# A gated mix of a state-space scan and a long convolution: issue order and buffer places planned by a list schedule in the builder, in place of tile pools and the library's scheduler

## The chip, the cores and the metric

The kernel runs on one core of one Trainium2 chip. The metric is the device time of the whole program in microseconds (us); smaller is better. Every number below comes from runs on such a chip or from the profile of one of them. A profiled execution has a "span", which is about 2 us shorter than the device time.

The core has five engines that issue independently. PE multiplies matrices (PEld is its weight load, which overlaps the multiplying), DVE is the vector engine, ACT the scalar engine, POOL a general engine that is slower at the elementwise work here (a 128x1024 bf16 multiply takes about 2.2 us on POOL and 0.68 us on DVE), and SP issues DMA transfers. In the traces each engine works its instructions off in the order in which they were put into its queue: two kernels below that have the same plan show the same 595 DVE instructions in the same order, and likewise for PE, ACT and SP. "POOL's queue" or "SP's queue" also stands for the DMA queue that this engine feeds. "Granted clock" (PEclk) is the share of full speed that PE was allowed.

## The reference

The inputs are `x`, `k`, `v` of 2048 × 1024 in bf16 (the argument `q` is ignored; `x` takes its place), the scan's parameters, and a convolution kernel of length 2048 for each of 1024 channels. Condensed, it computes:

```python
g = sigmoid((x * gate_w).sum(-1, keepdims=True))
# a: diagonal complex recurrence, P = 1024 states
Bu = x @ B_bar^T
h  = Lam_bar * h + Bu[t]          # for t in range(2048)
a  = 2 * real(h @ Cmat^T) + x * Dskip
# b: 4-tap shift convolution, product, long convolution of length 2048 by FFT
kv = shift_conv(k, shift_k) * v
b  = x * (causal_conv(kv, ssm_k) + kv * ssm_D)
out = g * a + (1 - g) * b
```

## The kernel before

The work has three kinds of pieces.

- **Scan**, 8 blocks of 128 states: prepare the block of B (`prep`), multiply it with x for odd and even rows (`gemm_u`), rotate, scan and rotate back on DVE (`rot`), then recover the odd rows on PE (`odd`). Each finished block of states, "H", two pieces of 512 KB, is stored to DRAM.
- **Convolution**, 8 units of 128 channels: a four-tap product on DVE (`kv_steps`), then a three-stage DFT on PE (`stage1`, `spec`, `inverse`), a complex `product` on DVE in the middle, and `final`, whose result is multiplied by x·(1−g) and stored to DRAM as `pB`.
- **Outputs**, 16 row tiles × 2 halves of the columns ("dh"): 16 matmuls each of H with C, then two DVE instructions that add x·Dskip and pB. Half 0 needs the convolution of units 0 to 3 alone, half 1 that of units 4 to 7.

PSUM, the matmul's result memory, is one pool with two 2-bank buffers for the scan (`psS`) and two for the convolution (`psB`). SBUF is a set of tile pools. The two halves of the program are Python generators. They are interleaved by a weight, and the library's scheduler settles each engine's final order.

```python
psum = ctx.enter_context(tc.tile_pool(name="psum", bufs=2, space=bass.MemoryType.PSUM))
pX = tc.tile_pool(reuse_waits="tile", name="pX", bufs=1, side="right")     # xT: all of x, transposed
...
def prep(pi, bn):
    dg = sp.tile([128, 6, 128], BF16, name="dg", bufs=3)
    for j, cf in enumerate(dcoef):                                         # six DVE instructions
        TS(out=dg[:, j, :], in0=ident, scalar1=col(cf, pi), scalar2=None, op0=ALU.mult)
...
# at the end of the scan: the right-hand pools are closed, a new one is opened in their place
pK.__exit__(None, None, None)
pS.__exit__(None, None, None)
pX.__exit__(None, None, None)
pC = tc.tile_pool(reuse_waits="tile", name="pC", bufs=1, side="right")
...
for pi in order:
    load_CT(0, pi)                                                         # two DMA transposes of C each
    Hs[pi] = cp.tile([128, NC, 2, 2, CW], BF16, name=f"Hr{pi}")
    for c in range(NC):
        nc.sync.dma_start(out=Hs[pi][:, c].rearrange("p a b s -> p (a b s)"), in_=h_scr[pi, c])
...
# one output tile
nc.gpsimd.tensor_tensor(out=xn, in0=xn, in1=dsk[:, ds_], op=ALU.mult)      # POOL
...
STT(out=pb, in0=xn, scalar=gc, in1=pb, op0=ALU.mult, op1=ALU.add)          # DVE
STT(out=ot, in0=ps[:, ti, :], scalar=gc, in1=pb, op0=ALU.mult, op1=ALU.add)
...
TOT_S, TOT_C = 190.0, 123.0
for w in sg:                                                               # the interleaving
    done_s += w
    while cg is not None and done_c < TOT_C * done_s / TOT_S:
        ...
```

## Time and profile before

The kernel before took 605.7 us (median of its first 3 runs, 603.29 to 607.32). These line numbers help with the profiles:

| piece | line before | line after |
|---|---|---|
| `prep`, PE | L235 | L750 |
| `gemm_u` | L261 | L785 |
| `odd` | L313 | L855 |
| DFT stage 1 / spec / inverse / final, PE | L563 / L573 / L593 / L617 | L633 / L647 / L673 / L695 |
| complex product, DVE, four instructions | L582, L583, L585, L586 | L660 to L663 |
| x·(1−g), POOL | L608 | L687 |
| x·Dskip, POOL | L429 | L961 |
| output matmuls; the DVE pair after them | L434; L440, L441 | L982; L970, L988 |

The page gives the busy time of each engine and its share of the span, then the span in 40 equal slices, with the busy share of each slice in tenths.

```profile
PE 463.6 (77%) x2720; PEld 244.4 (40%) x2720; DVE 351.7 (58%) x636; ACT 250.3 (41%) x278; POOL 132.9 (22%) x98
...
PE   0554896988799878978979938646826698879996
...
DVE  2967699395935788597698792232201372723432
...
PEclk9977897998899998998999989679757889898999
DMA  9996932622229216566386194168983454644331
```

No engine is full. In slices 26 to 31 (377 to 468 us) PE and DVE are both low, and the granted clock is low with PE. The same span can be cut at four events: the last odd step (363.9 us), the first output matmul (425.6 us), the last convolution matmul (516.9 us) and the end. The table by stretches gives the window, its length, the busy time and instruction count of PE, PEld, DVE, ACT and POOL, and then clock, DMA share and GB/s.

```profile
20.00:364.00 344.00, 283.88 (x1785) 155.73 (x1785) 262.80 (x479) 198.21 (x220) 76.03 (x48) 0.92 0.57 126
364.00:426.00 62.00, 40.16 (x311) 26.59 (x310) 17.32 (x29) 36.17 (x37) 3.79 (x2) 0.83 0.58 149
426.00:517.00 91.00, 62.66 (x290) 28.81 (x289) 29.35 (x39) 11.85 (x12) 21.84 (x16) 0.82 0.62 166
517.00:604.00 87.00, 76.94 (x336) 33.20 (x335) 34.51 (x46) 0.00 (x0) 23.31 (x20) 0.95 0.39 112
```

In the joint stage (first line) neither PE (83%) nor DVE (76%) is full. The 62 us between the last odd step and the first output matmul hold only convolution. The chain of waits, followed back from the end, says what the output stage waited for. Its first line is by engine ("SPq" is SP's sequencer), its second by line of the kernel.

```profile
PE 16%; SPq 10%; DMA 3%; issue 3%; DVE 2%; ACT 1%; POOL 0%; DVEq 0%; ACTq 0%; POOLq 0%
PE psS L434 15%; SPq L406 6%; SPq L600 2%; SPq L414 1%; DVE ot L441 1%; DMA xs<-in_A_x_dram 1%; DMA xn<-in_A_x_dram 1%; DVE pb L440 1%; DMA pb<-pB_scr 1%; DMA CT<-in_A_C_im_dram 0%; POOL xn L429 0%; ACT qq L597 0%; PE psB L593 0%; PE psB L573 0%; SPq L442 0%
```

L406 is the DMA transpose of C and L414 the reload of H. Both sit in SP's queue and can start only when the scan's pools are closed. (The chain reaches back over about a third of the span, to 396.61 us.)

### The profile page before, as it was taken

To read this page: it belongs to the slowest core of one execution; us is meant where nothing else is said; L and a number is where in the kernel's file an instruction comes from. 1 tells how busy PE (TensorE), PEld (TensorE's weight loads), DVE (VectorE), ACT (ScalarE), POOL (GpSimd) and SP (SyncE) were. 2 spreads that over 40 slices of the span, in tenths; PEclk is the share of its full clock that TensorE was granted. 3 is DMA by queue.
4 is the path that set the end of the run, shared out by engine and by line. 5 is a ranking of instruction groups with operands and counts; after the bars stand their busy time and mean duration, and the time that the engine had idled before them with its cause. 6 is when DMAs were issued, how large, how long until landed. Compare 5 with 4: busy or idle time off the path is not lost. (4 is left out here: it accounts for less than half of the span.)

```text
span 603.7 us, 7373 instructions
## 1 busy us (share of the span) xinstructions
PE 463.6 (77%) x2720; PEld 244.4 (40%) x2720; DVE 351.7 (58%) x636; ACT 250.3 (41%) x278; POOL 132.9 (22%) x98
## 2 busy tenths in 40 slices
PE   0554896988799878978979938646826698879996
PEld 0222553634465434634635615424402244333442
DVE  2967699395935788597698792232201372723432
ACT  2446693824396515845845736427300022000000
POOL 1820460304031310220120110110002451413330
PEclk9977897998899998998999989679757889898999
DMA  9996932622229216566386194168983454644331
GB/s 148 192 203 140 183 73 60 173 38 105 45 78 183 45 36 188 114 118 189 78 214 131 40 262 123 46 175 223 332 248 101 123 149 101 166 110 129 106 113 52
DMA packets 182723, 80.48 MB, mean 133 GB/s; under 512 B 147740, under 2 KB 176412, under 8 KB 182688
## 3 DMA queue, kind: packets, MB, share of 16 engines
q1 hardware_dynamic: 175032, 75.55, 53.3%
q0 software_dynamic: 1280, 4.20, 2.4%
q10 hardware_dynamic: 6376, 0.28, 0.9%
q8 instruction: 21, 0.34, 0.2%
q14 instruction: 14, 0.11, 0.1%
HBM read 33.85 MB, written 20.98 MB: 91 GB/s over the span
## 5 line engine op out<-in xcount | busy, mean ns | idle before, releaser
L434 PE MATMUL psS<-CT,Hr 128*128 128x512 bf16 x512 | 125.2, 403 | 30.8 <-DVE ot L441 20.8
L261 PE MATMUL psS<-xT,BT 128*128 128x512 bf16 x512 | 129.3, 393 | 7.1 <-ACT Hc L315 3.3
L434 PEld LDWEIGHTS <-Hr 128*128 128x128 bf16 x512 | 51.9, 102 | 101.3 <-issue 43.1
L576 ACT CAST kv<-psB 128x1024 bf16<-128x1024 f32 x64 | 65.1, 1032 | 29.3 <-PE psB L575 24.3
L261 PEld LDWEIGHTS <-BT 128*128 128x128 bf16 x512 | 50.2, 101 | 63.8 <-issue 17.9
L608 POOL TENSOR_TENSOR xs<-xs,omgj 128x1024 bf16<-128x1024 bf16 x16 | 35.4, 2213 | 149.0 <-DMA xs<-in_A_x_dram 110.1
L440 DVE SCALAR_TENSOR_TENSOR pb<-xn,gcols,pb 128x512 bf16<-128x512 bf16 x32 | 26.9, 848 | 70.3 <-POOL xn L429 37.8
L565 ACT CAST z<-psB 128x1024 bf16<-128x1024 f32 x64 | 62.5, 1029 | 12.6 <-PE psB L563 12.6
L429 POOL TENSOR_TENSOR xn<-xn,dsk 128x512 bf16<-128x512 bf16 x32 | 37.6, 1177 | 128.7 <-DMA xn<-in_A_x_dram 115.4
L597 ACT CAST qq<-psB 128x1024 bf16<-128x1024 f32 x32 | 32.7, 1026 | 78.6 <-PE psB L595 43.4
L582 DVE TENSOR_TENSOR t<-kv 128x1024 bf16<-128x1024 bf16 x32 | 25.1, 784 | 67.8 <-ACT kv L576 67.7
L573 PE MATMUL psB<-z,fC 128*128 128x512 bf16 x128 | 50.3, 393 | 7.3 <-ACT z L565 4.6
L272 ACT CAST Hc<-psS 128x1024 bf16<-128x1024 f32 x32 | 32.3, 1011 | 39.9 <-PE psS L261 14.7
L441 DVE SCALAR_TENSOR_TENSOR ot<-psS,gcols,pb 128x512 bf16<-128x512 f32 x32 | 24.0, 749 | 30.3 <-PE psS L434 28.9
L235 PE MATMUL psS<-dg,Bnr 128*128 128x256 bf16 x64 | 18.0, 309 | 30.4 <-DVE mask L463 20.2
L593 PE MATMUL psB<-pp,gC 128*128 128x256 bf16 x128 | 33.0, 292 | 10.8 <-DVE xs L619 5.2
L313 PE MATMUL psS<-Hc,dg 128*128 128x512 bf16 x64 | 24.6, 437 | 20.3 <-DVE Hc L305 19.7
L553 DVE TENSOR_TENSOR acc<-acc,tmpj 128x1024 bf16<-128x1024 bf16 (+3 forms) x48 | 35.5, 739 | 0.9
L574 PE MATMUL psB<-z,fS 128*128 128x256 bf16 x128 | 35.7, 279 | 0.0
L575 PE MATMUL psB<-z,fN 128*128 128x256 bf16 x128 | 35.7, 279 | 0.0
L315 ACT CAST Hc<-psS 128x1024 bf16<-128x1024 f32 x16 | 16.5, 1032 | 43.4 <-PE psS L313 43.4
L244 POOL TENSOR_SCALAR frt<-iota_row,phn 128x512 f32<-128x512 f32 x8 | 18.8, 2345 | 64.2 <-ACT tbc L251 52.7
(166 smaller groups left out, 727.3 us busy)
## 6 DMA issues: line engine op xcount, KB each, us to landing
zb<-qq SPq DMA_DIRECT2D x128, 64.0 KB
h_scr<-Hc SPq DMA_DIRECT2D x16, 512.0 KB
Hr<-h_scr SPq DMA_DIRECT2D x16, 512.0 KB
ka<-in_B_ssm_k_dram SPq DMA_DIRECT2D x8, 512.0 KB
xs<-in_A_x_dram SPq DMA_DIRECT2D x16, 256.0 KB
kv_scr<-acc SPq DMA_DIRECT2D x8, 512.0 KB
va<-kv_scr SPq DMA_DIRECT2D x8, 512.0 KB
pB_scr<-xs SPq DMA_DIRECT2D x16, 256.0 KB
```

Of the source, the lines that this page charges most:

```text
L261: nc.tensor.matmul(ps[:, ri, :], lhsT=BT[:, d, ri, :], rhs=xT[d][:, par, c0:c0 + CW], start=(d == 0), stop=(par == 1 and d == ND - 1))
L429: nc.gpsimd.tensor_tensor(out=xn, in0=xn, in1=dsk[:, ds_], op=ALU.mult)
L434: nc.tensor.matmul(ps[:, ti, :], lhsT=Hs[pi][:, a // 4, par, ri, (a % 4) * 128:(a % 4 + 1) * 128], rhs=CT[dh, pi][:, ri, :], start=(i == 0 ...
L553: TT(out=acc[:, lo:hi], in0=acc[:, lo:hi], in1=tmpj[:, 0:hi - lo], op=ALU.add)
L565: nc.scalar.copy(z[:, :, w, :, 64 * q:64 * q + 64].rearrange("p k r (g c) -> p k r g c", c=8), ps.rearrange("p g (k r c) -> p k r g c", r= ...
L573: nc.tensor.matmul(ps[:, i], lhsT=fC[:, k2, :], rhs=zz, start=True, stop=False)
L574: nc.tensor.matmul(ps[:, i, :, 0, :], lhsT=fS[:, k2, :], rhs=zz[:, :, 1, :], start=False, stop=False)
L575: nc.tensor.matmul(ps[:, i, :, 1, :], lhsT=fN[:, k2, :], rhs=zz[:, :, 0, :], start=False, stop=True)
L576: nc.scalar.copy(kv[:, 2 * h:2 * h + 2], ps)
L593: nc.tensor.matmul(ps[:, i], lhsT=gC[:, k2, :], rhs=pp[:, i], start=True, stop=False)
L597: nc.scalar.copy(qq, ps)
L608: nc.gpsimd.tensor_tensor(out=xs, in0=xs, in1=omgj[:, gs].unsqueeze(2).to_broadcast([128, 8, CH]), op=ALU.mult)
```

## The change

The intent is to fix the issue order of every engine and the place of every buffer in the builder. Code no longer issues instructions as it runs. It records operations with an engine, a cost in us written by hand, what they read and write, and a priority. A list schedule then simulates the five engines. Whenever an engine becomes free, it takes the ready operation with the lowest priority number whose buffers can be placed. The buffers are 21 slabs of 8 KB per partition, divided into 2 KB quarters, and four PSUM buffers that all stages share. The result is emitted with the library's own reordering switched off.

With this come smaller changes:

- The last two of the eight H blocks stay in SBUF (`NKEEP=2`).
- The six diagonals of a block are made by one POOL instruction.
- B loads and the H traffic go to POOL's DMA queue.
- Output loads and stores are taken two row tiles at a time.
- The output operations state that half 0 needs convolution units 0 to 3 only.

The diff replaces nearly the whole body; this is its core, with cuts.

```diff
+class _Plan:
+    SLAB = 8192
+    def op(self, eng, dur, fn, r=(), w=(), prio=0.0, dma=None): ...      # record, with dependences from r and w
+    def schedule(self, free0):
+        ...
+                    cand = sorted((o for o in waiting[e] if o.ready <= now + 1e-9), key=lambda o: (o.prio, o.idx))
+                    for o in cand:
+                        ...
+                        if not take(o):                                  # places its buffers, or the next candidate
+                            continue
+                        o.start = now
+                        if o.dma is None:
+                            o.end = now + o.dur
+                            efree[e] = o.end
+        ...
+        return sorted(self.ops, key=lambda o: (o.start, o.idx))
...
-    psum = ctx.enter_context(tc.tile_pool(name="psum", bufs=2, space=bass.MemoryType.PSUM))
+    NSLAB, NPS = 21, 4
+    slabs = [slabp.tile([128, 4096], BF16, name=f"slab{i}") for i in range(NSLAB)]
+    psums = [psum.tile([128, 1024], F32, name=f"ps{i}") for i in range(NPS)]
...
-            for j, cf in enumerate(dcoef):
-                TS(out=dg[:, j, :], in0=ident, scalar1=col(cf, pi), scalar2=None, op0=ALU.mult)
+            op("POOL", 1.5, lambda: G.tensor_tensor(out=dg.ap, in0=ident.unsqueeze(1).to_broadcast([128, 6, 128]),
+                                                    in1=dco[:, pi, :].unsqueeze(2).to_broadcast([128, 6, 128]),
+                                                    op=ALU.mult), w=[dg], prio=pr - 5)
...
-        pK.__exit__(None, None, None)
-        pS.__exit__(None, None, None)
-        pX.__exit__(None, None, None)
-        pC = tc.tile_pool(reuse_waits="tile", name="pC", bufs=1, side="right")
+            op("POOL", 2.3, lambda: G.tensor_tensor(out=xn.ap, in0=xn.ap,
+                                                    in1=dsk[:, ds_].unsqueeze(1).to_broadcast([128, 2, 512]), op=ALU.mult),
+               r=[xn], w=[xn], prio=pr - 8)
+            dma("SP", 0.9, lambda: [pb.ap], lambda: [rows(pB_scr)], [(e_pB, (u, h)) for u in range(4 * dh, 4 * dh + 4) for h in range(2)], [pb], pr - 6)
...
+    ZBCAP, NKEEP, HCAP, QB = 1, 2, 5, "POOL"
+    sg = s5(lambda x: 30.0 + 1.45 * x)                                    # priorities of the scan and the outputs
+    next(sg)
+    conv(lambda x: 35.0 + 2.6 * x)                                        # priorities of the convolution
+    for _ in sg:
+        pass
+    order = pl.schedule({"DVE": 14.0, "ACT": 14.0})
+    with tc.manual_schedule():
+        pl.emit(order, slabs, psums)
```

## The prediction

> **What bounds the kernel now.** No engine is full: the page's busy table gives PE 463.6 us of 603.7 (77%), DVE 351.7 (58%), ACT 250.3 (41%); the DMA engines are 53% occupied. The time is lost in three places.
>
> 1. Joint stage, 20 to 396 us (table by stretches): scan GEMMs and convolution together. DVE is busy 271 of 376 us, PE 305, ACT 218, granted clock 0.91. DVE and PE wait for each other in turn: the waits view has DVE before L582 waiting for ACT 41.5 us, before L281 30.6 us; PE before L313 (the odd step) for DVE 19.7 us.
> 2. Changeover, 396 to 450 us: PE 32 of 54 us, DVE 12.6, DMA 89% occupied. The right-hand pools are closed and reopened, then 32 transposes of C (1.2 us each on SP's queue) and 16 reloads of H, 512 KB each. The chain of waits runs along SP's queue here (L406, L414, L600); the first output matmul starts at 425.6 us.
> 3. Output, 450 to 604 us: PE waits for DVE's L441 20.8 us, DVE's L440 for pB reads and for POOL 70 us.
>
> **Full-clock PE work.** In dense runs the trace spaces matmuls of 512, 256, 128 columns by 0.216, 0.11, 0.056 us. All matmuls together (the count doesn't change): about 390 us.
>
> **What the change does.** Arithmetic is the same. Six DVE diagonals (about 0.34 us each, 16 us in all) become one POOL multiply per block; two of eight H blocks stay in SBUF, so four stores and four reloads of 512 KB vanish; H and B traffic moves from SP to POOL's queue; output loads and stores are paired, halving their issues. PSUM's four 2-bank buffers serve both halves instead of two each. Above all, order: shared slabs let the output stage begin while convolution still runs, without the changeover.
>
> The new PE order has, at full clock: 5 us before the first GEMM; 248 us to the last odd step; 6 us up to the first output matmul; 75 us of outputs mixed with the remaining convolution; 55 us of outputs alone. Up to the last rotation DVE has, with the trace's durations, about 285 us after a 14 us head; ACT 217 us. So the joint stage becomes DVE-bound. My estimate: 15 + 285/0.88 = 339 us, then 6 to 10 us of changeover, 130/0.96 = 136 us, and 10 to 15 us of stalls and tail: about 500 us.
>
> The Trainium skill, "TensorE: Matmul & The Clock Gate", Part 1, says the clock is released by recent activity. The trace agrees: 0.71 where PE was busy 17 of 30 us, 0.88 to 1.00 where it was busy 27 of 30. A denser PE should raise the mean from 0.90 to about 0.95.
>
> **Predicted: 500 us, 468 to 540 in 8 of 10. Faster by over 2%: 0.93; within 2%: 0.04; slower: 0.03.**
>
> **What would show it.** PE busy share above 85%, clock 0.94 or more; DVE above 85% in the joint stage, which ends by 345 us; no stretch like 396 to 450; first output matmul before 360 us; the last 60 us nothing but output matmuls; the chain of waits mostly PE and DVE, with SP's queue under 5%.
>
> **What would make it wrong.** All queues are fixed in the order of a model: one late DMA holds back everything behind it, on SP's queue above all (291 rows, 8 lanes, zb's 128 pieces waiting for ACT). POOL, with more work, may slow DVE (L582 took 0.78 us against 0.68 for its twin L583) and send its DMA late. Slab reuse may add waits across engines. If the joint stage keeps DVE at 75%, it lasts 395 us and the total is about 550.

## The result and the profile after

The changed kernel took 514.04 us (median of 4 runs, 511.82 to 521.75, the highest slow) beside 604.89 us for the kernel before, with a fourth run added. The ratio is 0.8483, with a 95% interval of 0.8431 to 0.8535. Here and below a ratio is the mean time of one kernel's fast runs over the mean of the other's fast runs of the same rounds, so it is not quite the ratio of the quoted medians, which are over all four runs. Its output is correct, and its profiled run has a span of 511.1 us.

The page of the kernel after:

```profile
PE 427.8 (84%) x2720; PEld 236.9 (46%) x2720; DVE 381.4 (75%) x595; ACT 248.0 (49%) x278; POOL 155.7 (30%) x121
...
PE   0239596979979997999679989997799999599996
...
DVE  2917499999999998989999999885337466426443
...
PEclk9999997899989999999999999999989999889999
DMA  9969659137747399389539924998578667233331
```

The same 2720 matmuls take 36 us less of PE's time, mostly because the granted clock rose from a mean of 0.904 to 0.971. The clock records hold only full and half speed here, and PE's busy time under half speed fell from 76.4 to 21.5 us; at full speed that work would have taken half as long, so I estimate that this accounts for 27 of the 36 us. DVE's busy time *rose* by 30 us, although DVE has fewer instructions. The fall in the middle is gone. The table by stretches, cut at the same four events (347.1, 356.7, 451.2 us and the end):

```profile
20.00:347.00 327.00, 283.57 (x1933) 164.92 (x1934) 290.25 (x446) 212.31 (x235) 107.61 (x88) 0.97 0.71 161
347.00:357.00 10.00, 7.28 (x75) 5.40 (x73) 7.46 (x8) 7.76 (x10) 4.16 (x2) 1.00 0.78 122
357.00:451.00 94.00, 81.47 (x461) 41.64 (x460) 46.80 (x57) 23.82 (x25) 23.35 (x11) 0.95 0.63 139
451.00:511.00 60.00, 55.45 (x257) 24.95 (x255) 26.90 (x33) 0.00 (x0) 13.19 (x6) 0.98 0.35 106
```

| part of the span, us | before | after | gain |
|---|---|---|---|
| start to last odd step | 363.9 | 347.1 | 16.8 |
| last odd step to first output matmul | 61.7 | 9.6 | 52.1 |
| first output matmul to end | 178.0 | 154.4 | 23.7 |
| sum | 603.7 | 511.1 | 92.6 |

(The gains are worked out from unrounded event times.) Cut this way, more than half of the gain lies at the changeover. But the first output matmul is a movable cut, since what is left of the convolution can run before it or after it. The firmer figure is the time from the last odd step to the end: 239.8 us before, 164.0 after, a gain of 76 us. Not all of the new time is well used: the joint stage gained only 17 us, though DVE is now busy 89% of it. The chain of waits, by engine, no longer has SP's queue in it to speak of. Followed in order of time, its last long piece is one dense run of 256 output matmuls:

```profile
PE 23%; ACT 3%; DVE 2%; DMA 2%; issue 1%; SPq 1%; DVEq 0%; ACTq 0%
...
451.15 55.31 PE ps L982 x256
```

**What the added DVE time is.** These are the groups of the last instruction of the complex product, on the same 128x512 tiles, before and then after. The columns after "x32" are the shortest, the median and the longest duration in ns, and the first and last start.

```profile
L586 DVE TENSOR_TENSOR pp<-t x32: 410/419/1484, 76.7 to 501.9; 128x512 bf16<-128x512 bf16 x32
```

```profile
L663 DVE TENSOR_TENSOR slab<-slab x32: 407/416/2703, 83.3 to 429.2; 128x512 bf16<-128x512 bf16 x32
```

The median did not move, but some instances take up to 2.7 us. The timeline of the kernel after shows when. Its columns are the start, the length, and the engine with its instruction; POOL comes first, then DVE.

```profile
140.01 4.52 POOL L687 TENSOR_TENSOR slab<-slab,omgj 128x1024 bf16<-128x1024 bf16 x2 [0.58 <-DMA slab<-in_A_x_dram]
...
145.10 1.48 POOL L738 TENSOR_TENSOR slab<-ident,dco 128x768 bf16<-128x768 bf16 x1
...
139.80 0.68 DVE L660 TENSOR_TENSOR slab<-slab 128x1024 bf16<-128x1024 bf16 x1
140.40 2.38 DVE L661 TENSOR_TENSOR slab<-slab 128x1024 bf16<-128x1024 bf16 x1
142.71 2.11 DVE L662 TENSOR_TENSOR slab<-slab 128x512 bf16<-128x512 bf16 x1
144.74 2.13 DVE L663 TENSOR_TENSOR slab<-slab 128x512 bf16<-128x512 bf16 x1
```

While POOL runs two multiplies of some 2.26 us each (4.52 us for both, to 144.53 us), the two DVE instructions beside them take 2.38 and 2.11 us instead of about 0.68 and 0.42. The next one, on DVE from 144.74 us, falls on the 1.48 us multiply that makes the diagonals, which POOL started at 145.10 us.

The Trainium skill says why, in "SBUF — State Buffer", section "Who interferes with whom". A DVE instruction with two SBUF inputs takes its second input through a read interface that it shares with POOL (there called GpSimd); according to the section "SBUF: two separate sides", whichever starts first gets it for the whole instruction, and "the other fully blocks". A DVE instruction with one SBUF input, outside certain modes, is not affected. The trace agrees in the main. The output instruction L988, which has one input in PSUM, took a mean of 695 ns beside POOL instructions and 709 ns without; L970, with two SBUF inputs, took 1482 against 670 ns (own times, as defined below). The trace does not show that the first to start wins: the record of L663 above begins 0.36 us before that of POOL's multiply, and it is DVE that is held up.

To add this up, I took each DVE instruction's own time (its end minus the later of its start and the end of the DVE instruction before it). From this I took off the median of the same line and shape when no POOL instruction was running. Over the instructions that overlapped POOL, this excess is 22.7 us before and 61.6 us after, 44.8 us of it in the joint stage. This is a computation from the trace, not a view of it. Most of the rise is not new work on POOL. Beside the multiplies by x·(1−g) and Dskip, which both kernels have, the excess went from 12.8 to 39.7 us, as they now fall on a busier DVE; the diagonals, which are new on POOL, account for 9.4 us.

### The profile page after: what moved, and what is told of

The parts are those of the page before. It is cut to its first block, busy times and chain, and to the rows that moved or that the text cites. A ratio compares the mean times of both kernels' runs of the same rounds, so it can differ in the third digit from the quotient of the medians.

```text
span 511.1 us, 7329 instructions
## 1 busy us (share of the span) xinstructions
PE 427.8 (84%) x2720; PEld 236.9 (46%) x2720; DVE 381.4 (75%) x595; ACT 248.0 (49%) x278; POOL 155.7 (30%) x121
## 5 line engine op out<-in xcount | busy, mean ns | idle before, releaser
L785 PE MATMUL ps<-slab,slab 128*128 128x512 bf16 x512 | 118.4, 386 | 6.8 <-ACT slab L897 3.7
L982 PE MATMUL ps<-slab,slab 128*128 128x512 bf16 x496 | 111.3, 382 | 1.4 <-DMA slab<-in_A_C_im_dram 0.9
L785 PEld LDWEIGHTS <-slab 128*128 128x128 bf16 x512 | 50.7, 99 | 64.8 <-issue 12.3
L651 ACT CAST slab<-ps 128x1024 bf16<-128x1024 f32 x64 | 63.2, 1034 | 34.7 <-PE ps L649 34.5
L982 PEld LDWEIGHTS <-slab 128*128 128x128 bf16 x512 | 50.4, 99 | 62.1 <-issue 4.6
L961 POOL TENSOR_TENSOR slab<-slab,dsk 128x1024 bf16<-128x1024 bf16 x16 | 35.6, 2225 | 105.5 <-DMA slab<-in_A_x_dram 66.6
L636 ACT CAST slab<-ps 128x1024 bf16<-128x1024 f32 x64 | 61.5, 1053 | 6.2 <-PE ps L633 6.2
L678 ACT CAST slab<-ps 128x1024 bf16<-128x1024 f32 x32 | 32.7, 1027 | 58.9 <-PE ps L675 36.6
L988 DVE SCALAR_TENSOR_TENSOR slab<-ps,gcols,slab 128x512 bf16<-128x512 f32 x32 | 23.4, 745 | 47.6 <-PE ps L982 39.6
L800 ACT CAST slab<-ps 128x1024 bf16<-128x1024 f32 x32 | 32.4, 1012 | 37.6 <-PE ps L785 25.2
L647 PE MATMUL ps<-slab,fC 128*128 128x512 bf16 x128 | 49.0, 383 | 1.2 <-ACT slab L636 1.2
L687 POOL TENSOR_TENSOR slab<-slab,omgj 128x1024 bf16<-128x1024 bf16 x16 | 32.9, 2062 | 50.4 <-DMA slab<-in_A_x_dram 43.2
L970 DVE SCALAR_TENSOR_TENSOR slab<-slab,gcols,slab 128x512 bf16<-128x512 bf16 x32 | 29.5, 963 | 14.3 <-DMA slab<-pB_scr 14.3
L633 PE MATMUL ps<-tab,slab 128*128 128x128 bf16 x512 | 34.2, 219 | 6.2 <-ACT slab L800 2.6
L620 DVE TENSOR_TENSOR slab<-slab,slab 128x1024 bf16<-128x1024 bf16 (+3 forms) x48 | 37.3, 777 | 1.7
L633 PEld LDWEIGHTS <-slab 128*128 128x128 bf16 x512 | 30.8, 98 | 10.0 <-issue 7.1
L649 PE MATMUL ps<-slab,fN 128*128 128x256 bf16 x128 | 35.2, 275 | 0.0
L648 PE MATMUL ps<-slab,fS 128*128 128x256 bf16 x128 | 35.2, 275 | 0.0
```

Of the source, the lines that this page charges most:

```text
L620: TT(out=acc.ap[:, lo:hi], in0=acc.ap[:, lo:hi], in1=tmp.ap[:, 0:hi - lo], op=ALU.add)
L633: PE_.matmul(ps.ap[:, i, :], lhsT=a.ap[:, 8 * q + i, :], rhs=t1v[:, hh * 128:(hh + 1) * 128], start=True, stop=True)
L636: op("ACT", 1.03, lambda: A.copy(z.ap[:, :, w, :, 64 * q:64 * q + 64].rearrange("p k r (g c) -> p k r g c", c=8), ps.ap.rearrange("p g (k ...
L647: PE_.matmul(ps.ap[:, i], lhsT=fC[:, k2, :], rhs=zz, start=True, stop=False)
L648: PE_.matmul(ps.ap[:, i, :, 0, :], lhsT=fS[:, k2, :], rhs=zz[:, :, 1, :], start=False, stop=False)
L649: PE_.matmul(ps.ap[:, i, :, 1, :], lhsT=fN[:, k2, :], rhs=zz[:, :, 0, :], start=False, stop=True)
```

## The experiments

Each kernel ran in four executions, beside runs of the kernel before on the same chip. All were correct except the first POOL experiment.

### Where the order pays: outputs held back

The outputs of half 0 wait for all eight units of the convolution instead of the first four.

```diff
-[(e_pB, (u, h)) for u in range(4 * dh, 4 * dh + 4) for h in range(2)]
+[(e_pB, (u, h)) for u in range(NU) for h in range(2)]
```

> The changed kernel, planned so that the first half of the outputs waits for all eight convolution units instead of four; correct result. Rival C (the gain comes from running outputs and convolution together, so that PE has output matmuls while ACT and DVE finish the convolution): the time rises by 25 us or more, to over 540 us. Theory A (the gain at the changeover is that C and H are loaded while other work still runs, not that matmuls of the two stages alternate; 28 us of PE work of the convolution remain at the last odd step, ACT-paced about 41 us, then 113 us of outputs): 500 to 522 us.

It took 540.22 us, ratio 0.8905 (0.885 to 0.896), against 0.8483 for the change as it is. Its table by stretches, cut at its last odd step, its first output matmul (also the end of its convolution) and the end:

```profile
20.00:349.00 329.00, 287.80 (x1934) 166.32 (x1935) 287.01 (x443) 213.25 (x236) 110.35 (x89) 0.96 0.70 155
349.00:424.00 75.00, 34.91 (x276) 22.44 (x275) 24.19 (x37) 31.11 (x33) 7.67 (x4) 0.77 0.72 127
424.00:541.00 117.00, 112.00 (x513) 50.32 (x511) 50.75 (x65) 0.00 (x0) 30.13 (x14) 0.98 0.35 108
```

The joint stage is the same length as in the changed kernel. The remainder of the convolution, alone, takes 75 us for 35 us of PE's time, at a granted clock of 0.77. I had expected this remainder to take about 41 us and was wrong. The convolution alone, a chain of PE, ACT, DVE and DMA steps, kept PE busy for less than half of the stretch, and the clock was low in the same stretch. Run together, the remainder and the outputs take 164 us (347 to 511) instead of 192 us (349 to 541), while the kernels differ by 26 us. So mixing outputs into the convolution is worth about 26 us of the 91 us gained. Here the time between the last odd step and the first output is 75 us, longer than in the kernel before, and still the kernel is 65 us faster than that one: this is why the 52 us of the table above are not a cause by themselves.

### What the fixed order is worth: the library's order put back

The same recorded operations are emitted in the same sequence into the same slabs, but the library's scheduler may reorder each engine.

```diff
-    with tc.manual_schedule():
-        pl.emit(order, slabs, psums)
+    pl.emit(order, slabs, psums)
```

> Correct result: the changed kernel's buffers and emission sequence, but the issue order of each engine is left to the library's own scheduler, as in the kernel before. Theory D (the fixed issue order is the larger part of the 91 us; the library's order costs waits even with the new places): 545 us or more. Rival E (the places are what mattered: slabs free of stage boundaries, early loads of C and H; any sensible order will do): 505 to 525 us.

It took 553.53 us, ratio 0.9146 (0.9082 to 0.9209). Its events, in us, are last odd step 384.8, first output 390.6, last convolution matmul 504.6 and end 551.7. Two of its stretches, the joint stage and the changeover:

```profile
20.00:385.00 365.00, 291.37 (x1944) 167.93 (x1944) 276.94 (x449) 215.05 (x235) 116.09 (x93) 0.94 0.65 147
385.00:391.00 6.00, 5.84 (x65) 4.50 (x63) 2.95 (x6) 6.00 (x7) 0.00 (x0) 1.00 0.41 92
```

The changeover is 6 us here too, and the stretch from the last odd step to the end takes 166.9 us, against 164.0 with the fixed order and 239.8 before. So nearly all of the 76 us gained there does not need the fixed order. It comes from what the builder does apart from it: places that need no closing of pools, early loads of C and H, and outputs mixed with convolution. What the fixed order adds is 39 us (553.5 to 514.0). It lies in the joint stage, which is 38 us longer here, with DVE busy 76% of it instead of 89%. That is 545 us or more, as theory D has it, but not its reason: 39 of 91 us is not the larger part. How the rest divides between slabs, pairing and early loads was not separated.

### What true costs are worth: flat costs in the plan

Every operation but the DMA transfers counts as 1.5 us in the plan; the emitted instructions are the same.

```diff
     def op(self, eng, dur, fn, r=(), w=(), prio=0.0, dma=None):
+        if dma is None:
+            dur = 1.5
```

> Correct result: the plan is made with 1.5 us for every compute step instead of its calibrated cost (0.46 to 6 us), transfers unchanged. If calibrated costs are needed for a good fixed order, 540 us or more; if dependences, priorities and buffer limits already give the order, 505 to 525 us.

The three fast runs took 560.72 to 563.14 us, and the median of all four is 562.09; the ratio is 0.9266 (0.9194 to 0.9338). The profiled run was a slow one, so no line of it is used. A fixed order planned with wrong costs is 48 us worse than the one with the hand-written costs, and no better than the library's order (553.5 us). Fixing the order gains nothing here without costs close to the truth.

### Two parts that bring little: kept blocks, and POOL's DMA queue

```diff
-    ZBCAP, NKEEP, HCAP, QB = 1, 2, 5, "POOL"
+    ZBCAP, NKEEP, HCAP, QB = 1, 0, 5, "POOL"      # first run: no H block kept in SBUF
+    ZBCAP, NKEEP, HCAP, QB = 1, 2, 5, "SP"        # second run: B and H traffic back on SP's queue
```

> Correct result: all eight H blocks go to HBM and back, as in the kernel before (four stores and four loads of 512 KB more, on POOL's queue). The reloads run while convolution remains, so if keeping two blocks is only a small help, 508 to 522 us; if the reloads pace the changeover, they add about 4 x 2 us and the first output is delayed: 522 to 535 us.

> Correct result: loads of B and stores and loads of H issued by SP as in the kernel before, not by POOL. Theory A adds: DVE excess beside POOL's DMA issues (8.3 us) goes away, DVE busy falls by 5 to 10 us. Against it, SP's in-order queue gets 40 more entries, of which 24 wait on compute. I expect 512 to 530 us; under 508 us would mean that POOL's issuing itself was a cost on the critical path.

Keeping no block took 516.18 us, ratio 0.8548 (0.8463 to 0.8632, one run of the four slow). The first output comes 27 us later (383.8 instead of 356.7), yet the end is at 511.3 us instead of 511.1. Convolution fills the gap, and what is put off then runs denser. So the first output was delayed, which I had tied to 522 us or more, and it cost next to nothing. This is a shift of work within a stage that ends at the same time. B and H traffic on SP's queue took 512.84 us, ratio 0.8466 (0.8409 to 0.8523), which is the same time, although DVE's busy time fell by 15.8 us to 365.6 (I had expected 5 to 10) and the last odd step ended 12.5 us earlier, at 334.6 us. What was won there was lost again behind it. These two parts of the change are neutral.

### What POOL's multiplies cost: leave them out

The POOL multiplies by 1−g (L687) and by Dskip (L961) are not issued. The plan still counts them, so the planned order is unchanged. The result is wrong.

```diff
-            op("POOL", 2.25, lambda: G.tensor_tensor(out=xs.ap, in0=xs.ap, ...
+            op("POOL", 2.25, lambda: None,
...
-            op("POOL", 2.3, lambda: G.tensor_tensor(out=xn.ap, in0=xn.ap, ...
+            op("POOL", 2.3, lambda: None,
```

> Wrong result on purpose: the changed kernel with its 32 POOL multiplies (L687, L961, 68.5 us of POOL) left out, same plan, same order on the other engines. Theory A (POOL's two-input multiplies hold up DVE instructions that run beside them; 62 us of DVE's 381 us busy are such excess, 35 us of them beside these two lines): DVE busy falls by 25 to 40 us to about 345 us, and because DVE paces the joint stage the time falls by 10 to 20 us, to 494 to 504. Rival B (DVE's long records are only bookkeeping of waits, the plan's pace is set by PE and the fixed order): DVE busy falls, but the time stays at 510 to 516 us.

It took 501.52 us, ratio 0.8282 (0.8226 to 0.8338). Its page line, and then its timeline on DVE at the same instructions of the complex product:

```profile
PE 428.0 (86%) x2720; PEld 237.8 (48%) x2720; DVE 339.6 (68%) x595; ACT 247.8 (50%) x278; POOL 86.0 (17%) x89
```

```profile
142.59 0.68 DVE L661 TENSOR_TENSOR slab<-slab 128x1024 bf16<-128x1024 bf16 x1
143.19 0.42 DVE L662 TENSOR_TENSOR slab<-slab 128x512 bf16<-128x512 bf16 x1
143.53 0.42 DVE L663 TENSOR_TENSOR slab<-slab 128x512 bf16<-128x512 bf16 x1
```

The three instructions that took 2.1 to 2.4 us are back at 0.42 to 0.68 us, and DVE's busy time falls by 41.8 us with the same 595 instructions in the same order (I had expected 25 to 40). The time falls by only 12.5 us. Of the 41.8 us, 25 lie in the joint stage, and its end moved by 9 us, from 347.1 to 337.9; the rest of DVE's time came back as waits. That is evidence against the simple statement that DVE bounds the joint stage.

### A version with no POOL arithmetic, correct

If POOL's arithmetic is what hurts, it should be moved and the order planned anew.

- The diagonals are made by ACT (copy with a scale).
- The small tables are made by DVE.
- The convolution's result is stored unscaled, by an ACT copy.
- In the output stage ACT multiplies pB by 1−g.
- DVE then forms (Dskip·g + pB) and multiplies it by x, which serves both terms, so the 16 loads of x beside `final` are gone.

```diff
-            op("POOL", 2.25, lambda: G.tensor_tensor(out=xs.ap, in0=xs.ap, in1=omgj..., op=ALU.mult), ...
-            op("DVE", 1.22, lambda: TT(out=xs.ap, in0=ps.ap..., in1=xs.ap, op=ALU.mult), ...
+            op("ACT", 1.03, lambda: A.copy(xs.ap, ps.ap.rearrange("p a g c -> p (a g) c")), r=[ps], w=[xs], prio=pr)
...
-            op("POOL", 1.5, lambda: G.tensor_tensor(out=dg.ap, ...
+            def dgf():
+                for j in range(6):
+                    A.activation(out=dg.ap[:, j, :], in_=ident, func=ACT.Copy, scale=dco[:, pi, j:j + 1])
+            op("ACT", 1.4, dgf, w=[dg], prio=pr - 5)
...
-            op("POOL", 5.9, f, r=[e_iota], w=[f_, q_], prio=pr - 5)        # tables; f used G.tensor_scalar, G.tensor_tensor
+            op("DVE", 1.4, f, r=[e_iota], w=[f_, q_], prio=pr - 5)         # f now uses TS, TS, TT
...
-            op("POOL", 2.3, lambda: G.tensor_tensor(out=xn.ap, in0=xn.ap, in1=dsk..., op=ALU.mult), ...
+            def sc():
+                for ti in range(2):
+                    A.activation(out=pb.ap[:, ti, :], in_=pb.ap[:, ti, :], func=ACT.Copy, scale=col(omgj, gi[ti]))
+            op("ACT", 1.3, sc, r=[pb, e_gate], w=[pb], prio=pr - 5)
...
-                    STT(out=pb.ap[:, ti, :], in0=xn.ap[:, ti, :], scalar=col(gcols, gi[ti]), in1=pb.ap[:, ti, :], ...
+                    STT(out=pb.ap[:, ti, :], in0=dsk[:, ds_], scalar=col(gcols, gi[ti]), in1=pb.ap[:, ti, :], ...
+                TT(out=pb.ap, in0=pb.ap, in1=xn.ap, op=ALU.mult)
```

> Correct result, no tensor arithmetic left on POOL: tables on DVE (10 us), diagonals on ACT, the convolution's result stored unscaled through ACT, 1-g applied by ACT per output row, the products with x and D in three DVE instructions. Theory A (POOL holds up DVE for 62 us, most of it where DVE paces the kernel): DVE busy falls to 330 to 345 us and the time to 475 to 500 us. Rival B (pace set elsewhere): 505 us or more, as ACT gets 40 us of work more.

It took 474.69 us (472.41 to 476.08), ratio 0.7824 (0.7772 to 0.7875), and the result is correct. It beats both kernels: it is 131 us below the kernel before and 39 us below the changed one. DVE's busy time, 322.8 us, is below the 330 to 345 that I had expected, as is the time, if barely. Its page line, its joint stage, and the last instruction of its complex product:

```profile
PE 421.5 (89%) x2720; PEld 235.4 (50%) x2720; DVE 322.8 (68%) x619; ACT 295.5 (63%) x374; POOL 28.8 (6%) x55
```

```profile
20.00:311.00 291.00, 275.13 (x1930) 162.31 (x1929) 249.39 (x462) 233.74 (x290) 24.38 (x43) 0.99 0.72 168
```

```profile
L663 DVE TENSOR_TENSOR slab<-slab x32: 414/417/419, 74.9 to 390.3; 128x512 bf16<-128x512 bf16 x32
```

The shortest and the longest instance of that instruction now differ by 5 ns; the excess over all of DVE is 0.2 us. The joint stage ends at 310.8 us instead of 347.1, and PE is busy 95% of the stretch from 20 us to there. This version changes several things at once, so the next two runs put back the suspect alone.

### The suspect alone: 32 idle POOL instructions added to the last version

Each instruction reads a constant (`dsk`) and writes a buffer of its own that nothing else uses, and nothing waits for it. In one kernel it multiplies two SBUF inputs, in the other it scales one.

```diff
+    scr = parm.tile([128, D], BF16, name="scr")
+    def dose(key, prio):
+        op("POOL", 2.25, lambda: G.tensor_tensor(out=scr, in0=dsk, in1=dsk, op=ALU.mult), r=[(e_dose, key)], prio=prio)
# in the second kernel instead:
+        op("POOL", 2.25, lambda: G.tensor_scalar(out=scr, in0=dsk, scalar1=2.0, scalar2=None, op0=ALU.mult), r=[(e_dose, key)], prio=prio)
...
+            dose(("f", u, h), pr)                       # one beside each final: 16
+            dose(("o", dh, par, a2), pr - 4)            # one beside each output pair: 16
```

> Correct result: the kernel without POOL arithmetic (0.7824 of the kernel before) with 32 idle POOL multiplies put back, 128x1024 bf16, two SBUF inputs, on buffers that nothing else uses; planned where the old ones stood, order of PE, DVE, ACT and SP otherwise the same. Theory A (a POOL instruction with two SBUF inputs holds up DVE): DVE busy rises from 323 by 20 to 40 us, the time by 5 to 15 us (ratio 0.79 to 0.807). Rival F (the gain came from the rearranged arithmetic and the shorter chain at the convolution's end, not from a free POOL): DVE busy and time within 5 us of it.

> The same dose with one SBUF input: 32 POOL tensor_scalar instructions of the same output. Theory A, after the trace of the changed kernel, where POOL's one-input lines L766 and L767 went with 5 us of excess in 33 us and its two-input lines with 48 us in 80: DVE busy rises by less than 10 us and the time by less than 4 us. If any POOL work holds up DVE alike, as much as with two inputs.

| kernel | us | ratio (95%) | POOL time of the added ones | DVE busy | DVE excess beside them |
|---|---|---|---|---|---|
| without | 474.69 | 0.7824 (0.7772–0.7875) | – | 322.8 | – |
| two inputs | 507.46 | 0.8366 (0.8336–0.8395) | 66.2 us | 376.9 | 55.1 us |
| one input | 475.63 | 0.7863 (0.7814–0.7911) | 92.4 us | 342.7 | 20.8 us |

(The profile with one input is of the slowest of its four runs, 481.01 us.)

The page line, the added group on POOL (busy us and mean ns of one, then POOL's idle time before it) and the last product instruction on DVE (shortest, median, longest), first for two inputs, then for one:

```profile
PE 428.9 (85%) x2720; PEld 239.5 (47%) x2720; DVE 376.9 (75%) x619; ACT 296.1 (59%) x374; POOL 95.2 (19%) x87
...
L494 POOL TENSOR_TENSOR scr<-dsk 128x1024 bf16<-128x1024 bf16 x32 | 66.2, 2068 | 2.0
...
L670 DVE TENSOR_TENSOR slab<-slab x32: 410/416/2108, 74.5 to 423.2; 128x512 bf16<-128x512 bf16 x32
```

```profile
PE 423.1 (88%) x2720; PEld 235.8 (49%) x2720; DVE 342.7 (72%) x619; ACT 295.8 (62%) x374; POOL 121.3 (25%) x87
...
L494 POOL TENSOR_SCALAR scr<-dsk 128x1024 bf16<-128x1024 bf16 x32 | 92.4, 2888 | 2.2
...
L670 DVE TENSOR_TENSOR slab<-slab x32: 410/416/1257, 78.9 to 397.5; 128x512 bf16<-128x512 bf16 x32
```

Instructions that nobody needs cost the kernel 33 us when they have two SBUF inputs, and 1 us when they have one, although the second set kept POOL busy for longer. PE, DVE, ACT and SP execute the same instructions in the same order in all three kernels. So it is not POOL's time or its queue that costs, but what its reading takes from DVE. By DVE's busy time that is (376.9 − 322.8)/66.2 = 0.82 us of DVE for each us of POOL with two inputs, and (342.7 − 322.8)/92.4 = 0.22 with one. With two inputs I had expected 20 to 40 us more on DVE and 5 to 15 us more of time; it was 54 and 33. I had expected one-input instructions to add less than 10 us to DVE; they added 20, and only my expectation for the time held.

The trace with one input also shows that DVE is not held up for the whole of POOL's instruction:

```profile
155.28 2.78 POOL L494 TENSOR_SCALAR scr<-dsk 128x1024 bf16<-128x1024 bf16 x1
...
155.26 1.62 DVE L848 TENSOR_TENSOR slab<-slab,slab 128x1024 bf16<-128x1024 bf16 x1
156.92 0.42 DVE L849 TENSOR_TENSOR slab<-slab 128x512 bf16<-128x512 bf16 x1
157.26 0.42 DVE L850 TENSOR_TENSOR slab<-slab 128x512 bf16<-128x512 bf16 x1
```

L848 takes 1.62 us instead of 0.68. L849 and L850, with two SBUF inputs each, take their usual 0.42 us, though the one-input POOL instruction runs on to 158.06 us.

There is one caveat. As nothing waited for them, 21 of the 32 instructions ran from 290 us on, most of them back to back, to 353 us with two inputs and to 366 us with one, so 33 us is not exactly the cost of the original ones. Nor did the two sets run beside the same work of DVE. The twelve that ran before 300 us stood at nearly the same places in both kernels; there the excess is 21.2 us for 23.7 us of POOL (0.89) with two inputs and 13.2 for 34.7 (0.38) with one. So one input costs clearly less, but not nothing, and 0.22 is partly a matter of where the late ones ran. The changed kernel's own trace points the same way. Of its 61.6 us of excess, 55.8 us lie beside two-input POOL lines that are busy for 92 us (L687, L961, L738, L768), and 4.5 us beside one-input lines that are busy for 33 us (L766, L767).

### Starting sooner: two attempts that lost

In the changed kernel the first GEMM starts at 41.7 us, against 25.0 before. First attempt, on the changed kernel: k and v of unit 0 are transposed between the odd and the even rows of x, so that DVE has convolution work sooner.

```diff
-... [(xT[d], par)], -1000 + d, transpose=True)
+... [(xT[d], par)], (-1000 if par else -500) + d, transpose=True)
-        kvprep(0, prio(-12))
+        kvprep(0, -700)
```

> Correct result: the changed kernel with the two transposes of k and v of unit 0 planned between the odd and the even rows of x, instead of after all 16 transposes. If DVE's total work paces the joint stage, giving DVE work 15 us earlier (it is busy 23 of 40 us between 20 and 60 us) brings the time down by 5 to 12 us, to 502 to 509. If PE or DMA pace it, the same time, 510 to 518 us, since even rows of x arrive 8 us later.

Second attempt, on the version without POOL arithmetic: the preparation of the second block has to wait for the odd-row GEMMs of the first block.

```diff
-                op("PE", 8 * MM(256), f, r=[bn, dg], w=[ps], prio=pr)
+                op("PE", 8 * MM(256), f, r=[bn, dg] + ([e_first] if pi == 1 else []), w=[ps], prio=pr)
...                                                      # e_first is written by the second odd-row GEMM of block 0
```

> Correct result: the kernel without POOL arithmetic, with one dependence added to the plan: the second block's projections may not be issued before the first block's odd-row GEMMs, because in the trace those GEMMs stand behind a B load that lands at 28.5 us. If PE's total paces this kernel, the first GEMM starts by 27 us instead of 31.7 and the time falls by 2 to 6 us (466 to 473 us); the earlier try of the like kind (k and v first) came out 14 us worse, so a reshuffled plan may also cost 5 to 15 us.

The first took 527.88 us, ratio 0.8708 (0.8647 to 0.8769), which is 14 us slower than the change and outside both of the ranges that I had named. The second took 485.54 us, ratio 0.8031 (0.7982 to 0.808, one run of the four slow), which is 11 us slower than the version it started from, as the text had said it might be. Its first GEMM did start at 21.9 us instead of 31.7, but its joint stage ended at 315.1 us instead of 310.8. In the first, the planner itself computed a shorter span than for the changed kernel (497.1 against 501.5, the model's numbers, not measurements), and the chip gave a longer one. For the version without POOL arithmetic it computed 508.5, which is 7 us more than for the changed kernel, and the chip took 39 us less: the model's costs are fixed numbers, which do not tell when POOL holds up DVE.

An edit at one place changes the plan at all others. Why these two plans run worse I did not find. What they show is that the plan's own estimate does not rank plans that lie within about 10 us of each other, and that the time of the first GEMM does not bound this kernel.

### Better costs in the plan

The costs of the version without POOL arithmetic are set from its own trace (ACT evictions 0.93 instead of 1.03 us, product 1.9 instead of 2.35, scan 2.32 instead of 2.8, and so on).

```diff
-            op("DVE", 2.35, f, r=[kv], w=[t1, t2, pp], prio=pr)
+            op("DVE", 1.9, f, r=[kv], w=[t1, t2, pp], prio=pr)
...                                                      # 18 more costs in the same way
```

> Correct result: the kernel without POOL arithmetic, replanned with the costs that its own trace shows (DVE 10 to 20% shorter where POOL no longer holds it up, ACT evictions spaced 0.92 us instead of 1.03). As flat costs made the plan 48 us worse, true costs might make it better: 460 to 472 us. If the plan's quality is by now limited by what the model has not (landing times of DMA, PE's clock) or by chance, 470 to 485 us.

It took 474.94 us, ratio 0.7847 (0.7807 to 0.7888), which is no change. Costs that are off by a tenth or a fifth, most of them in the same direction, do no harm here; flat ones do.

One more experiment was meant and could not be run: the four PSUM buffers divided again into two and two. The plan found no order for it until other buffer allocations were changed as well, so it would not have tested PSUM sharing alone. That share stays open.

## Why the prediction was right, and where not

The predicted time was 500 us (468 to 540), and faster by over 2% with 0.93; 514.04 us was measured. Point by point:

- **The changeover vanishes, first output before 360 us: right.** The changeover took 9.6 us (6 to 10 predicted), and the first output matmul came at 356.7 us. The stretch behind the last odd step, of which it is the start, holds the largest part of the gain, 76 us, and the run with the library's order shows that this needs the new builder but not the fixed order. The changeover alone is not what was gained: with no kept block it took 37 us and the kernel ended at the same time.
- **Joint stage to about 339 us, DVE above 85%: nearly right in the number, half right in the reason.** It ended at 347.1 us (345 was the limit I named), and DVE was 89% busy. But 45 us of that busy time is excess beside POOL. I had put DVE's work up to there at about 285 us, and 296 us were measured from 14 us on; without the excess it would have been about 251. That the sums came so close is in part luck: the work was less than I thought, and a loss that I had not costed filled the gap. Without POOL's arithmetic the joint stage ends at 310.8 us with DVE at 249.4 of 291 us. And the stage is not simply bound by DVE: taking 25 us of DVE time away from it, in an unchanged order, moved its end by only 9 us (347.1 to 337.9).
- **Outputs: 130/0.96 = 136 us, then 10 to 15 us of stalls and tail, so up to 151; measured 154.4.** The term was somewhat too small. My full-clock PE work of about 390 us was too small by about the 64 matmuls of `final`, whose moving operand is 512 columns wide; counted again it is 403.5 us, also an estimate from the spacing of dense matmuls.
- **Clock: right.** I predicted 0.94 or more; 0.971 was measured. The Trainium skill, "TensorE: Matmul & The Clock Gate", Part 1, ties the granted clock to recent activity of PE. The trace agrees: 0.77 where the held-back convolution ran alone (PE busy 35 of 75 us), 0.98 in the dense output stretch after it.
- **PE above 85% busy: just missed, 84%.** The higher clock also shortens PE's busy time (463.6 to 427.8 us).
- **SP's queue under 5% of the chain: right,** 1% after 10%. But the move of traffic to POOL's queue had nothing to do with the time: with SP's queue the kernel takes 512.84 us.
- **The last 60 us hold output matmuls alone: right,** as the chain's 55.31 us at the end and ACT's 0.00 in the last stretch show.
- **"POOL, with more work, may slow DVE": named as a risk and not costed.** It was the largest thing left out. The excess went from 22.7 to 61.6 us, and the version without it is 39 us faster.
- **The change's own parts.** I had counted the moved diagonals as a gain for DVE (48 instructions of about 0.34 us each in the mean, 16 us). Moving them put eight two-input multiplies of 1.49 us on POOL, and beside these alone lie 9.4 us of excess on DVE, more than half of what the move was to save.

The separate experiments cannot be summed: held-back outputs (+26 us), library order (+39), flat costs (+48) and no POOL arithmetic (−39) overlap, because each one plans or orders everything anew.

## What to carry to other kernels

Where one stage must free its memory before the next can load, plan buffer places and loads across the boundary, and let the tail of one stage run beside the head of the next; here the stretch behind the boundary fell from 240 to 164 us, about 26 of the 76 us from mixing outputs into the rest of the convolution. In this kernel a fixed order was worth having only with costs near the truth (flat costs were no better than the library's order), and since two small edits made such a plan 11 and 14 us slower, each plan has to be measured. Before giving arithmetic to POOL to relieve a busy DVE, compare the shortest and the longest duration of the same DVE instruction: two-input POOL work took back 0.82 us of DVE for each of its own us, and moving it to ACT and DVE gained 39 us.

## What the Trainium skill lacked or had wrong

- "SBUF — State Buffer", section "Who interferes with whom", says that a POOL instruction which reads SBUF contends with a DVE instruction of two SBUF inputs. The runs agree (2.11 us instead of 0.42 us for one instruction). It makes no difference between POOL instructions with one and with two SBUF inputs, and does not say how much of POOL's time DVE loses. The runs show 0.22 and 0.82 us of DVE lost for each us of POOL (0.38 and 0.89 where both sets ran at nearly the same places). The page's section "SBUF: two separate sides" has the loser blocked for the whole instruction; beside the one-input POOL instruction of 2.78 us at 155.28 us, DVE instructions with two SBUF inputs took their usual 0.42 us in its second half.
- "GPSIMD Engine Reference", section "4.1 Engine selection", calls one-input elementwise work on POOL roughly line-rate and two-input work slower. Here it was the other way round for 128x1024 bf16: the one-input scaling took a mean of 2888 ns and the two-input multiply 2068 ns (spans on POOL are rough in the profile, but the ranges of the 32 instances of each do not overlap: 2769 to 3394 and 1893 to 2688 ns).
- I found no page on choosing between a fixed issue order and the library's scheduler, or on how exact a plan's costs must be. The runs show 39 us for the fixed order, 48 us lost with flat costs, and nothing gained from costs refined by a tenth or a fifth.
